# Local heads loaded as fp32 by the hardware queues, crossbar transposes from batch 3, P v with [v|1], and MoE tiles of 256 tokens

## The chip, the cores and the metric

The kernel runs on one core of one Trainium2 chip. The metric is the device time of one execution, in microseconds (us); lower is better. Two runs of the kernel before took 360.77 and 363.22 us, median 362.0 us. "Slow" means over 1.5% above the fastest run of the same kernel in the same series, and only fast runs are compared. TensorE's granted clock is given for each run, 1.0 being full speed.

In the lines of the profile, PE is a matmul on TensorE, PEld a weight load there, DVE is VectorE, ACT ScalarE, POOL GpSimd and SP the Sync engine; L203 is line 203 of the kernel. PSUM, in banks, is the memory that the matmuls write. "The crossbar" is the path by which a DMA transposes on the way (`dma_start_transpose`). "Cold" stands for TensorE at half clock.

The span of a profile (first to last instruction) is about 1.7 us shorter than the time of the same run, so spans are compared with spans and times with times.

## The reference

```python
# q, k, v: (8 batches, 8 heads, 576, 64) fp32
scores = q @ k^T / 8
local   (heads 0..3): 0 <= i - j < 32
strided (heads 4..7): 0 <= i - j and i % 32 == j % 32
attn = softmax(where(mask, scores, -1e9)) @ v
x = attn as (4608 tokens, 512)
h = x @ w_in                       # 512 -> 2048
out = where(h > 0, h, exp(min(h, 0)) - 1) @ w_out   # 2048 -> 512, fp32
```

The matmuls run in bf16. Strided heads are computed residue by residue (8 residues of 72 positions); local heads in blocks of 96 queries against 128 keys.

## The kernel before

All loads go through the GpSimd queue, which casts fp32 to bf16 on the way. Every pair of heads is transposed on TensorE, scored, masked and multiplied by v in "pieces"; one piece is dealt out with each step of the MoE (one tile of the first product, L347, and four matmuls of the second, L382).

```python
def load_qloc(b):                    # cast inside the DMA, GpSimd queue
    t = p_in.tile([RS, 2, NS, 2, D], BF16, tag="ql", name="ql")
    for h in range(HG):
        nc.gpsimd.dma_start(out=t[:, h // 2, :, h % 2, :],
                            in_=q[b, h].rearrange("(p s) d -> p s d", s=NS))
    return t
# ... load_str, load_kloc, load_vloc alike; load_batch calls qs, ks, vs, ql, kl, vl

def piece_T(P):                      # 14 to 16 TensorE transposes, two DVE copies
    for nm, dst in (("q", P.qT[:, 0:S]), ("k", P.kT[:, PRE:PRE + S])):
        ps = p_a.tile([128, S], BF16, tag="a", name="tp")
        # ... nc.tensor.transpose(ps[:, o:o + RS], src..., identity[0:RS, 0:RS])
        nc.vector.tensor_copy(dst, ps)

def piece_S(P, u, split=False):      # scores, exp on ScalarE, mask on DVE
    # ... nc.tensor.matmul(scs[z][...], lhsT=P.kT[...], rhs=P.qT[...])
    nc.scalar.activation(e[0:R], sc[0:R, :, 0:W], ACT.Exp, scale=scale)
    nc.vector.tensor_mul(pm, e, mask)

def piece_O(P, u, pm):               # sums by a matmul with ones, then P v
    nc.tensor.matmul(s_ps[x * D:(x + 1) * D, :], lhsT=ones, rhs=pm[:, x], ...)
    nc.tensor.matmul(o_ps[x * D:(x + 1) * D, i * LQ:(i + 1) * LQ], lhsT=v..., ...)
    # ... rc = exp(-ln(s_ps)) on ScalarE; xT = o_ps * rc on DVE

def l1(nb, m):                       # 128 of d_ff x 512 tokens
    for c in range(KC):
        nc.tensor.matmul(hps, lhsT=w_in_sb[:, cc, m * 128:(m + 1) * 128],
                         rhs=xT[:, cc, nb * CHUNK:(nb + 1) * CHUNK], ...)
    nc.scalar.activation(e, hps, ACT.Exp)
    nc.vector.tensor_scalar(e1, e, scalar1=1.0, scalar2=1.0, op0=ALU.min, op1=ALU.subtract)
    nc.vector.tensor_tensor(g[:, m, :], e1, hps, op=ALU.max)

# order of the start: batch 0's q, k; masks; batch 0's rest; w_in; load_batch(1); w_out;
# batch 0's pieces alone; then, for every MoE step, one piece of the following batches
for nb in range(NCH):
    for m in range(MC):
        if nb > 0: l2(nb - 1, m)
        if done < len(pieces): run_piece(pieces[done], ...); done += 1
        l1(nb, m)
        if loaded < B and done >= (loaded - 1) * PB + 4:
            batch_in[loaded] = load_batch(loaded); loaded += 1
```

The softmax here doesn't subtract the row's maximum and nothing guards it: scores larger than these inputs give would overflow.

## Time and profile before

| | before |
|---|---|
| time, median of 2 | 362.0 us |
| span of the profile | 361.1 us |
| TensorE busy | 329.1 us, 91% |
| first matmul | 6.5 us |
| first MoE tile starts | 36.3 us |
| one batch of attention beside the MoE (12 steps) | 29.85 us |

The page of the kernel before. The second line has the busy time of each engine and its share of the span. In the lower lines each digit is one fortieth of the span (9.0 us), in tenths of busy time; PEclk is the granted clock in tenths, and DMA the mean busy share of the DMA engines.

```profile
span 361.1 us, 6843 instructions
PE 329.1 (91%) x2656; PEld 161.5 (45%) x2656; DVE 243.8 (68%) x501; ACT 194.3 (54%) x377; POOL 92.3 (26%) x120
...
PE   1851986999999999999999999999999999999995
...
PEclk9999999899999999999999999999999999999999
DMA  6999999999959965992960111010111110021122
```

TensorE is at nine tenths from the eighth slice on (63 us): it is the bound, except at the start. The waits of TensorE in the kernel before (engine, line, awaited; then us in total, number of waits, longest):

```profile
PE tp L203 <- DMA qs<-in_q_dram: 18.4, 3, 9.4
PE tp L203 <- DMA ks<-in_k_dram: 3.6, 3, 1.4
```

Nearly all its waiting is for the strided q and k of the first batches. The timeline of TensorE in the steady part (start us, us, engine, line, operation, tiles, count) shows one step, with transposes, and the start of the next:

```profile
101.21 1.04 PE L347 MATMUL hps<-xT,w_in_sb 128*128 128x512 bf16 x4
102.08 1.03 PE L382 MATMUL ops<-w_out_sb,g 128*128 128x512 bf16 x4
103.04 0.31 PE L270 MATMUL s_ps<-pm,ones 72*64 72x288 bf16 x2
103.18 0.30 PE L279 MATMUL o_ps<-pm,vs 72*64 72x72 bf16 x8
103.41 0.43 PE L211 MATMUL tp<-identity,ql 72*128 72x72 bf16 x8
103.85 0.42 PE L211 MATMUL tp<-identity,kl 96*128 96x96 bf16 x6
104.11 1.03 PE L347 MATMUL hps<-xT,w_in_sb 128*128 128x512 bf16 x4
```

The step that starts at 101.21 has four matmuls of the first product, four of the second, two sums, eight P v matmuls, and then 14 transposes before the next step at 104.11. Read durations from start to start, since the ends of pipelined matmuls overlap: four 512-wide matmuls take 0.87 us (101.21 to 102.08). The busy time of the engines in twelve such steps (window, length, then busy time and instructions of PE, PEld, DVE, ACT and POOL, clock, DMA share, GB/s):

```profile
98.83:128.68 29.85, 29.72 (x286) 14.75 (x286) 23.78 (x49) 19.81 (x40) 10.28 (x13) 1.00 0.85 91
```

TensorE works 29.72 of 29.85 us. 96 MoE matmuls of 0.216 us are 20.7 us of it, so that attention costs 9.15 us a batch.

### The profile page before, as it was taken

The numbers are of one execution on the slowest core, as the hardware profiler recorded it, in microseconds if no ns is written. First come the engines' busy times: TensorE is split into PE (matmuls) and PEld (weight loads), VectorE is DVE, ScalarE is ACT, GpSimd is POOL, SyncE is SP. The second block draws the span as 40 slices with busy tenths as digits, with TensorE's granted clock in tenths as the row PEclk, the third lists the DMA queues.
The fourth block names the chain that finished last, engine by engine and source line by source line (L and its number), as shares of the span: only waits on it lengthen the run. The fifth ranks groups of instructions, "written<-read, shape, count | busy, mean of one in ns | idle before, by whom it ended". The sixth has DMA issues, their size and how long they took to land.

```text
span 361.1 us, 6843 instructions
## 1 busy us (share of the span) xinstructions
PE 329.1 (91%) x2656; PEld 161.5 (45%) x2656; DVE 243.8 (68%) x501; ACT 194.3 (54%) x377; POOL 92.3 (26%) x120
## 2 busy tenths in 40 slices
PE   1851986999999999999999999999999999999995
PEld 1630443454544544445454454444444444444442
DVE  2640797787877877777878777776666666666610
ACT  1650575667566666666666666664444433543411
POOL 7952843958507214510620000000000000000000
PEclk9999999899999999999999999999999999999999
DMA  6999999999959965992960111010111110021122
GB/s 91 113 178 178 107 199 158 99 159 152 142 93 102 96 101 72 87 114 63 119 48 29 31 31 31 29 32 29 46 44 30 34 55 29 29 59 31 30 71 76
DMA packets 88321, 29.03 MB, mean 80 GB/s; under 512 B 72672, under 2 KB 83680, under 8 KB 88288
## 3 DMA queue, kind: packets, MB, share of 16 engines
q0 software_dynamic: 82432, 19.14, 61.7%
q1 hardware_dynamic: 5856, 9.44, 9.1%
q8 instruction: 21, 0.34, 0.4%
q14 instruction: 12, 0.10, 0.1%
HBM read 38.21 MB, written 9.44 MB: 132 GB/s over the span
## 4 chain that ended last, share of the span: by engine, by line
PE 73%; DMA 12%; ACT 6%; POOL 4%; issue 2%; DVE 2%; ACTq 0%
PE ops L382 32%; PE hps L347 30%; DMA vs<-in_v_dram 5%; DMA ks<-in_k_dram 5%; PE tp L211 3%; PE tp L203 2%; PE sc L243 2%; ACT e L251 2%; ACT osb L387 2%; DMA vl<-in_v_dram 2%; DVE pm L259 2%; PE s_ps L286 1%; ACT ln L297 1%; PE s_ps L270 1%; POOL kl L85 1%
## 5 line engine op out<-in xcount | busy, mean ns | idle before, releaser
L347 PE MATMUL hps<-xT,w_in_sb 128*128 128x512 bf16 x576 | 151.4, 386 | 0.2
L382 PE MATMUL ops<-w_out_sb,g 128*128 128x512 bf16 x576 | 145.4, 379 | 0.0
L352 ACT ACTIVATE he<-hps 128x512 f32<-128x512 f32 x144 | 85.8, 596 | 103.7 <-PE hps L347 103.0
L382 PEld LDWEIGHTS <-g 128*128 128x128 bf16 x576 | 56.4, 98 | 68.0
L347 PEld LDWEIGHTS <-w_in_sb 128*128 128x128 bf16 x576 | 50.8, 99 | 53.3 <-issue 2.1
L251 ACT ACTIVATE e<-sc 72x576 bf16<-72x576 f32 (+1 forms) x60 | 38.3, 639 | 17.4 <-PE sc L243 17.4
L297 ACT ACTIVATE ln<-s_ps 128x288 f32<-128x288 f32 x64 | 26.3, 411 | 16.9 <-PE s_ps L270 8.7
L387 ACT COPY osb<-ops 128x512 f32<-128x512 f32 x36 | 21.1, 586 | 20.0 <-PE ops L382 20.0
L76 POOL DMA_DIRECT2D ql<-in_q_dram x32 | 27.2, 855 | 18.0 <-PE tp L211 6.6
L299 ACT ACTIVATE rc<-ln 128x288 f32<-128x288 f32 x64 | 28.4, 443 | 2.0
L85 POOL DMA_DIRECT2D kl<-in_k_dram x32 | 23.7, 758 | 19.7 <-DMA ks<-in_k_dram 5.5
L203 PE MATMUL tp<-identity,qs 72*128 72x72 bf16 x128 | 7.9, 213 | 18.4 <-DMA qs<-in_q_dram 18.4
L304 DVE TENSOR_TENSOR xT<-o_ps,rc 128x288 bf16<-128x288 f32 x32 | 14.6, 456 | 8.3 <-ACT rc L299 7.9
L309 DVE TENSOR_TENSOR xT<-o_ps,rc 128x288 bf16<-128x288 f32 x32 | 14.6, 457 | 7.8 <-ACT rc L299 5.0
L253 DVE TENSOR_TENSOR pm<-e,mask_s 72x576 bf16<-72x576 bf16 x32 | 14.5, 452 | 3.8 <-ACT e L251 2.4
L259 DVE TENSOR_TENSOR pm<-e,mask_l 128x576 bf16<-128x576 bf16 x32 | 14.6, 457 | 2.5 <-ACT e L251 0.5
L203 PEld LDWEIGHTS <-qs 72*128 72x128 bf16 x128 | 5.8, 108 | 19.9 <-DMA qs<-in_q_dram 18.7
L67 POOL DMA_DIRECT2D vs<-in_v_dram x8 | 5.7, 710 | 31.9 <-PE sc L243 31.6
L96 POOL DMA_DIRECT2D vl<-in_v_dram x8 | 9.6, 1197 | 11.8 <-PE tp L203 11.4
L286 PE MATMUL s_ps<-pm,ones 128*64 128x288 bf16 x64 | 10.6, 322 | 1.6 <-DVE pm L259 0.9
L203 PE MATMUL tp<-identity,ks 72*128 72x72 bf16 x128 | 7.9, 214 | 3.9 <-DMA ks<-in_k_dram 3.6
L291 PE MATMUL o_ps<-pm,vl 128*64 128x96 bf16 x192 | 10.6, 215 | 0.7 <-DMA vl<-in_v_dram 0.7
(343 smaller groups left out, 338.5 us busy)
## 6 DMA issues: line engine op xcount, KB each, us to landing
out_dram<-osb SPq DMA_DIRECT2D x32, 144.0 KB
qs<-in_q_dram POOLq DMA_DIRECT2D x8, 288.0 KB, 5.9
ks<-in_k_dram POOLq DMA_DIRECT2D x8, 288.0 KB, 7.7
vs<-in_v_dram POOLq DMA_DIRECT2D x8, 288.0 KB, 7.9
ql<-in_q_dram POOLq DMA_DIRECT2D x32, 72.0 KB, 6.3
kl<-in_k_dram POOLq DMA_DIRECT2D x32, 72.0 KB, 4.2
vl<-in_v_dram POOLq DMA_DIRECT2D x8, 288.0 KB, 5.5
w_in_sb<-in_moe_w_in_dram POOLq DMA_DIRECT2D x4, 512.0 KB, 10.9
```

Source lines behind the costliest of these rows:

```text
L76: nc.gpsimd.dma_start(out=t[:, h // 2, :, h % 2, :], in_=q[b, h].rearrange("(p s) d -> p s d", s=NS))
L85: nc.gpsimd.dma_start(out=t[:, h // 2, :, h % 2, :], in_=src[b, h].rearrange("(t p) d -> p t d", p=LQ))
L203: nc.tensor.transpose(ps[:, o:o + RS], src[:, P.g0 + x, 2 * sp * D:2 * (sp + 1) * D], identity[0:RS, 0:RS])
L251: nc.scalar.activation(e[0:R], sc[0:R, :, 0:W], ACT.Exp, scale=scale)
L259: nc.vector.tensor_mul(pm, e, mb.unsqueeze(1).to_broadcast([128, 2, W]))
L297: nc.scalar.activation(ln, s_ps, ACT.Ln)
L299: nc.scalar.activation(rc, ln, ACT.Exp, scale=-1.0)
L304: nc.vector.tensor_mul(dst, o_ps.rearrange(pat, z=2, sp=2), rc.rearrange(pat, z=2, sp=2))
L347: nc.tensor.matmul(hps, lhsT=w_in_sb[:, cc, m * 128:(m + 1) * 128], rhs=xT[:, cc, nb * CHUNK:(nb + 1) * CHUNK], start=(c == 0), stop=(c == ...
L352: nc.scalar.activation(e, hps, ACT.Exp)
L382: nc.tensor.matmul(ops, lhsT=g[:, m, kk * 128:(kk + 1) * 128], rhs=w_out_sb[:, m, :], start=(m == 0), stop=(m == MC - 1))
L387: nc.scalar.copy(o_sb, ops)
```

## The change

The intent was to take work off TensorE: the transposes of batches 3 to 7 go to the DMA crossbar, and the separate matmuls for the row sums go away by multiplying with [v|1] in the array's free columns. Local heads come as fp32 over the Sync and ScalarE queues in one load each and are cast on GpSimd. MoE tiles of 256 tokens (two 128-wide slices of d_ff in one PSUM bank) let the MoE begin when batch 0 alone is finished; 16 of these tiles run before batch 1's attention. The core of the diff:

```diff
-CHUNK = 512
+SUB = 256
+RP = 80
...
-    def load_qloc(b):
-        t = p_in.tile([RS, 2, NS, 2, D], BF16, tag="ql", name="ql")
-        for h in range(HG):
-            nc.gpsimd.dma_start(...)
+    def load_ql(b, eng):
+        eng.dma_start(out=ql32..., in_=q[b, 0:HG].rearrange("h (t p) d -> p (h t) d", p=LQ))
...
+    def dma_T(b, which):            # qs, ks, ql, kl -> qsT, ksT, qlT, klT
+        nc.sync.dma_start_transpose(out=out_.rearrange("p (c n) -> p c n", n=n), in_=in_)
...
+    def piece_O(b, hp, u, pm):      # two banks: [o|sum] and [sum|o]
+        o = [p_a.tile([128, W], F32, tag="a", name=f"o{x}") for x in range(2)]
+        for x, c, vt, mv in pv_terms(b, hp, u, pm):
+            nc.tensor.matmul(o[x][:, c], lhsT=vt[:, x * D:(x + 2) * D], rhs=mv, ...)
+        nc.scalar.activation(ln[lo], o[0][hi], ACT.Ln)
+        nc.scalar.activation(ln[hi], o[1][lo], ACT.Ln)
+        nc.scalar.activation(rc, ln, ACT.Exp, scale=-1.0)
+        x_out(b, hp, u, lo, o[0], rc)          # DVE multiply, 64 partitions
+        x_out(b, hp, u, hi, o[1], rc)
+    def piece_O2(b, hp, u, pm):     # sums apart, as before; batches 0 and 1
...
+    def l1(j, t, mode="A", spare=False):
+        for mm in range(2):
+            for c in range(KC):
+                nc.tensor.matmul(hps[:, mm], lhsT=w_in_sb[... stride 4 ...],
+                                 rhs=xT[:, c, r0:r0 + SUB], ...)
+        nc.scalar.activation(e, hps, ACT.Exp)
+        if mode == "B":
+            nc.scalar.activation(e1, hps, ACT.Relu)
+            nc.vector.scalar_tensor_tensor(gt, e, 1.0, e1, op0=ALU.subtract, op1=ALU.min)
+        else:
+            eng = nc.gpsimd if mode == "P" else nc.vector
+            eng.tensor_scalar(e1, e, scalar1=1.0, scalar2=1.0, op0=ALU.min, op1=ALU.subtract)
+            nc.vector.tensor_tensor(gt, e1, hps, op=ALU.max)
...
+    # start: batch 0's loads, casts, v casts on GpSimd, then w_in; batch 0's attention;
+    load_str(1, qs, q); load_str(1, ks, k); load_str(1, vs, v)
+    load_kl(1, nc.scalar); load_ql(1, nc.scalar); load_vl(1, nc.scalar)
+    # ... batch 1's casts on GpSimd; w_out
+    for n, (j, t) in enumerate(first):         # 16 tiles of batch 0
+        l1(j, t, mode="BP"[n % 2], spare=n % 3 == 2)
+    for it in att_T(1, "O2"):
+        do(it)
+    # ... then 128 steps "n": one tile of l1 and four matmuls of l2 each, with the attention
+    # of batches 2 to 7 dealt among them; START = {3: 22, 4: 34, 5: 50, 6: 67, 7: 84}
```

## The prediction

> **What bounds it now.** The page gives TensorE 91% busy, its 40 slices over 90% from about 62 to 356 us: TensorE-bound except at the ends. In the timeline after 242 us (MoE only) a 128x512 matmul starts every 0.216 us; 1152 make 248.5 us. In steady state (chain of waits, 98.83 to 128.68 us) twelve steps, one batch of attention, take 29.85 us; 96 MoE matmuls are 20.7, so attention costs TensorE 9.15 us a batch, 73 in all. Sum 322 of 361 us. The other 39: 6.5 before the first matmul, 4 after the last, the rest before 62 us, where the waits view names DMA (18.4 us for q, 3.6 for k, strided heads, behind the weights in the GpSimd queue) and matmuls run cold (four 512-wide ones 1.9 us, not 0.86).
>
> **TensorE.**
> - Transposes leave it for batches 3 to 7. A step without them takes 2.44 us, 1.73 of it MoE: score plus P v cost 0.71, eight 5.7 a batch, four transposes the other 3.45. 5 x 3.45 = 17 us saved.
> - P v with [v|1]: separate sum matmuls (0.12 to 0.15 us) go in 48 pieces of batches 2 to 7. The o_ps matmuls already take their serial time (six of 96 columns in 0.24 us), so full width adds nothing. About 5 us saved (0.10 each).
> - 256-token tiles: same columns, 576 more matmuls. The Trainium skill, "TensorE: Matmul & The Clock Gate", section "Wait — 56ns, not 53.3ns?", gives N / 2.4 GHz + about 2.5 ns; 0.216 us for 512 agrees. Estimate from it: +1.4 us. Weight loads now stride by four elements; transposes here reload 128-column weights every 0.03 us, so I expect them hidden under 0.109 us.
>
> Net -21 us, all on the critical path in steady state.
>
> **Other engines.** A batch, DVE loses 8 copies (0.45 us) and gains 8 output multiplies (0.457): even; ACT gains 8 Ln (0.41). Estimate per steady batch of 18 steps (about 35 us): DVE 31 us, ACT 29; DVE has 12% slack. GpSimd casts (eight a batch, about 1.2 us each, from 1.03 for 128x576) share its SBUF port with DVE (Trainium skill, "SBUF — State Buffer": an exclusive lock for the whole instruction; before's one 1.10 us DVE minimum among 0.42 us ones may be that). I allow 4 us of bubbles: DVE, PSUM banks (P v takes two of three), late transposes.
>
> **Startup.** Batch 0 starts later (first matmul near 11 us, after local q, k land as 256-byte pieces and are cast), then 16 MoE tiles of batch 0 need only w_in, then batch 1's attention runs with no MoE beside it (about 14 us for 9 of work). About 32 us of TensorE work done at 62 us, against 29 before: 3 gained. Larger runs for w_out and three queues may give 5 more. Tail unchanged.
>
> **Predicted time.** 362 - 21 - 3 - 5 + 4, rounded down: 334 us, range 318 to 352. Faster by over 2%: 0.86; within: 0.10; slower: 0.04.
>
> **What would show each step.** Transposes only of batches 0 to 2 in the groups; 18 steady steps near 35 us. 256-wide matmuls starting every 0.109 us when nothing waits; 0.12 or more means exposed strided weight loads. No s_ps after batch 1. TensorE continuously busy from about 60 us. No scores waiting for DMA transposes.
>
> **What would make it wrong.** Exposed strided weight loads (+10% is 12 us); crossbar transposes so slow that scores wait at each batch's start; stores stuck behind them in the Sync queue; DVE or ACT becoming the bound through strided output multiplies or GpSimd's lock; a startup slower than before because 256-byte fp32 loads come first.

## The result, and the profile after

The changed kernel took 387.56 us (386.77 and 388.35) against 362.0 us in the same series: the ratio is 1.070, 95% interval 1.060 to 1.080. A ratio is always the mean time of one kernel's fast runs over that of the other's of the same rounds, so it is not quite the ratio of the medians quoted. A faster kernel, 334 us, had been predicted; it is 7% slower than before.

The page of the changed kernel (one slice is 9.7 us):

```profile
span 386.6 us, 7373 instructions
PE 318.0 (82%) x2783; PEld 225.5 (58%) x2824; DVE 264.9 (69%) x488; ACT 221.7 (57%) x433; POOL 98.8 (26%) x108
...
PE   0575117676997779997999999999999999999995
...
PEclk9999658855899999999999999999999999999999
DMA  9789999005010996998919988995946111101111
```

TensorE did less (318.0 us busy, although much of the start ran at half clock; some matmul records are missing in this trace), and it stays under nine tenths in the first ten slices (97 us), where in before it is there from the eighth slice on (63 us). PEclk falls to five and six tenths in four of them. TensorE's waits in the changed kernel:

```profile
PE hps L316 <- DVE g L332: 15.4, 12, 9.5
PE tp L199 <- DVE qlb L116: 12.7, 1, 12.7
PE hps L316 <- ACT he L327: 7.2, 1, 7.2
```

The first wait is mainly one of 9.5 us for the activation of an early MoE tile; the second is the load and cast of batch 0 before the first matmul at 12.73 us; the third is one wait for ScalarE. The windows view of the changed kernel by stage (columns as in before): the start up to the main loop's step 0, steps 0 to 12, 12 to 18, 18 to 108, and the tail:

```profile
0.00:94.24 94.24, 46.02 (x496) 35.84 (x496) 45.52 (x79) 38.62 (x76) 49.49 (x52) 0.79 0.80 136
94.24:118.40 24.16, 22.97 (x172) 16.49 (x172) 15.53 (x31) 9.73 (x17) 1.31 (x2) 0.90 0.08 22
118.40:149.80 31.40, 25.66 (x245) 15.79 (x245) 19.31 (x40) 19.76 (x41) 9.18 (x11) 1.00 0.75 126
149.80:339.60 189.80, 181.59 (x1612) 128.97 (x1640) 161.17 (x300) 136.96 (x272) 38.84 (x44) 1.00 0.71 124
339.60:386.60 47.00, 41.74 (x268) 28.37 (x271) 23.39 (x42) 16.63 (x28) 0.00 (x0) 0.99 0.16 46
```

The granted clock in the start is 0.79 by this view, which overstates it: the trace has no clock record before 37.8 us, and the view takes that as full clock, but six transposes of 96 columns took 0.46 us there (12.73 to 13.19) against 0.26 in the steady part of before. The record itself has half clock from 41.2 to 61.7 us and from 75.4 to 99.2. (The start of before was cold as well, up to about 41 us: four 512-wide matmuls took 1.8 us at 36.32.) The main loop begins at 94.24 us. The work done by then (attention of batches 0 and 1 at 9.15 us each and 16 tiles at 0.87) is 32.2 us of TensorE at full clock. The kernel before has 28.7 us of it done when its 13th tile starts, at 62.27 us, and the other 3.5 would bring it to about 66 us. So the start costs 28 us more than in before, and the remaining 292.4 us are only some 3 us fewer than before's remaining 295. The difference of the spans, 25.5 us, is the sum of the two. There are two misses to explain, then: a start that grew, and a steady part that hardly shrank.

What ScalarE did when TensorE first waited for it, in the changed kernel's timeline (ACTq rows are DMA issues on ScalarE's queue; the bracket is the idle time before and what ended it):

```profile
30.25 6.98 ACTq L96 DMA_DIRECT2D ql<-in_q_dram  x1
37.32 3.92 ACTq L106 DMA_DIRECT2D vl<-in_v_dram  x1
41.28 2.99 ACTq L107 DMA_DIRECT2D vl<-in_v_dram  x1
44.32 0.60 ACT L324 ACTIVATE he<-hps 128x512 f32<-128x512 f32 x1 [14.00 <-issue]
```

The last attention activation ended near 30.3 us. The next, the exponential of the first MoE tile, ran at 44.32, after 14.00 us in which ScalarE's queue did nothing but issue the rest of batch 1's local loads. GpSimd in the same stretch (POOL rows):

```profile
41.86 0.82 POOL L116 CAST klb<-kl 96x768 bf16<-96x768 f32 x1 [12.04 <-DMA kl<-in_k_dram]
...
52.01 2.05 POOL L126 COPY vsx<-vs 72x1024 bf16<-72x1024 bf16 x2
54.01 3.87 POOL L331 TENSOR_SCALAR he<-he 128x512 bf16<-128x512 f32 x2
```

It waits for those loads until 41.86 us, casts and copies until 54.0, and only then runs the min/subtract of the first MoE tiles given to it, 1.94 us each, where VectorE takes 0.456. TensorE, whose PSUM banks wait to be emptied, stands still until 56.77 us.

The steady part of the changed kernel, in an undisturbed stretch (to be read against the timeline of before):

```profile
245.27 0.30 PE L220 MATMUL sc<-qsT,ksT 64*128 64x72 bf16 x8
245.50 1.07 PE L316 MATMUL hps<-xT,w_in_sb 128*128 128x256 bf16 x8
246.40 1.03 PE L356 MATMUL ops<-w_out_sb,g 128*128 128x512 bf16 x4
247.27 0.42 PE L266 MATMUL o<-pm,vsx 72*128 72x72 bf16 x8
247.53 1.04 PE L316 MATMUL hps<-xT,w_in_sb 128*128 128x256 bf16 x8
```

Eight 256-wide matmuls take 0.90 us (245.50 to 246.40), P v with [v|1] 0.26 (247.27 to 247.53), scores 0.23, and there are no transposes. That is as expected, and a step averages 2.04 us in such stretches; but steps 18 to 108 took 189.80 us, 2.109 each. At the starts of batches TensorE waits for chains of score, exponential, mask and P v.

### The profile page after: what moved, and what is told of

It is laid out like the page before. It is cut to its first block, busy times and chain, and to the rows that moved or that the text cites. A ratio compares the mean times of both kernels' runs of the same rounds, so it can differ in the third digit from the quotient of the medians.

```text
span 386.6 us, 7373 instructions
## 1 busy us (share of the span) xinstructions
PE 318.0 (82%) x2783; PEld 225.5 (58%) x2824; DVE 264.9 (69%) x488; ACT 221.7 (57%) x433; POOL 98.8 (26%) x108
## 4 chain that ended last, share of the span: by engine, by line
PE 56%; DVE 14%; ACT 9%; issue 5%; DMA 5%; POOL 4%; SPq 3%; ACTq 3%; DVEq 0%; POOLq 0%
PE hps L316 25%; PE ops L356 24%; DVE xT L244 3%; DMA vl<-in_v_dram 3%; PE sc L220 3%; DVE g L332 3%; POOL he L331 2%; ACT e L223 2%; DVE he L331 2%; ACT osb L361 2%; ACTq L96 2%; SPq L96 2%; PE o L266 1%; PE tp L199 1%; DMA qlT<-qlb 1%
## 5 line engine op out<-in xcount | busy, mean ns | idle before, releaser
L316 PE MATMUL hps<-xT,w_in_sb 128*128 128x256 bf16 x1152 | 156.1, 282 | 26.2 <-DVE g L332 15.4
L316 PEld LDWEIGHTS <-w_in_sb 128*128 128x128 bf16 x1152 | 124.0, 116 | 45.6 <-issue 24.3
L332 DVE TENSOR_TENSOR g<-he,hps 128x512 bf16<-128x512 bf16 x136 | 93.5, 687 | 31.4 <-POOL he L331 18.0
L331 DVE TENSOR_SCALAR he<-he 128x512 bf16<-128x512 f32 x128 | 58.3, 456 | 34.0 <-ACT he L324 32.7
L223 ACT ACTIVATE e<-sc 128x576 bf16<-128x576 f32 (+1 forms) x64 | 41.3, 646 | 19.7 <-PE sc L220 18.0
L244 DVE TENSOR_TENSOR xT<-o,rc 64x288 bf16<-64x288 f32 x48 | 32.2, 670 | 7.8 <-ACT rc L272 7.0
L116 POOL CAST klb<-kl 96x768 bf16<-96x768 f32 x14 | 11.9, 849 | 84.5 <-DMA kl<-in_k_dram 84.5
L269 ACT ACTIVATE ln<-o 64x288 f32<-64x288 f32 x48 | 19.6, 408 | 13.8 <-PE o L266 13.4
L240 DVE TENSOR_TENSOR xT<-o,rc 64x288 bf16<-64x288 f32 x48 | 21.8, 454 | 5.1 <-ACT rc L272 4.0
L270 ACT ACTIVATE ln<-o 64x288 f32<-64x288 f32 x48 | 19.4, 404 | 2.3 <-PE o L266 1.2
L126 POOL COPY vsx<-vs 72x1024 bf16<-72x1024 bf16 x16 | 17.6, 1129 | 1.6 <-DMA vs<-in_v_dram 1.6
L120 POOL CAST vlx<-vl 128x768 bf16<-128x768 f32 x16 | 14.1, 908 | 13.9 <-DMA vl<-in_v_dram 13.3
L331 POOL TENSOR_SCALAR he<-he 128x512 bf16<-128x512 f32 x8 | 15.8, 1994 | 5.9 <-ACT he L324 5.9
```

The costliest lines, as they stand in the source:

```text
L240: nc.vector.tensor_mul(xs[:, u * W:(u + 1) * W], o[pr], rc[pr])
L244: nc.vector.tensor_mul(dst, o[pr].rearrange(pat, b=3, s=NS), rc[pr].rearrange(pat, b=3, s=NS))
L269: nc.scalar.activation(ln[lo], o[0][hi], ACT.Ln)
L316: nc.tensor.matmul(hps[:, mm], lhsT=w_in_sb[:, c, (m // 4) * 512:(m // 4 + 1) * 512].rearrange("c (p mm) -> c mm p", mm=4)[:, m % 4], rhs= ...
L331: eng.tensor_scalar(e1, e, scalar1=1.0, scalar2=1.0, op0=ALU.min, op1=ALU.subtract)
L332: nc.vector.tensor_tensor(gt, e1, hps, op=ALU.max)
```

## The experiments

Eighteen kernels ran. All computed the right result but one, which is told. The medians and ranges quoted are of all runs of a kernel, the ratios of its fast runs alone; e10, e12, e13 and e14 have one slow run each, and e6, e7, e16 and e18 are told below. "Before" was run beside each; it took 361.2 to 362.7 us (medians) throughout. The "main loop's start" below is the time of the first tile of step 0 in the profile, 94.24 us in the changed kernel.

### The start: who issues, who computes

**e1_sp_loads**: batch 1's local loads are issued on the Sync queue.

```diff
-    load_kl(1, nc.scalar); load_ql(1, nc.scalar); load_vl(1, nc.scalar)
+    load_kl(1, nc.sync); load_ql(1, nc.sync); load_vl(1, nc.sync)
```

> Edit: only batch 1's three local fp32 loads are issued by the Sync engine instead of ScalarE. Theory A (two gates in a row: ScalarE held 14 us by issuing the loads, then the MoE tiles that go through GpSimd held until its casts end at 54 us): ScalarE is free at 30 us, but the second tile still waits for GpSimd, so the time stays within 5 us of 387.6 (383 to 388). Rival B (the 14 us on ScalarE is the whole loss of the startup): about 373. Rival C (startup is bound by the arrival of bytes): no change, 387.

Measured: 382.25 us (380.19 to 384.32), ratio 1.057 [1.051, 1.063], just below the range of theory A; the main loop starts at 87.7 us. The wait for ScalarE (7.2 us) is gone; in its place the first tiles wait 8.2 us for w_in, which now shares the DMA engines with the earlier loads, and 5.6 us at the next tiles for the activation that GpSimd does.

**e2_no_pool**: the first tiles do not use GpSimd for the activation.

```diff
-        l1(j, t, mode="BP"[n % 2], spare=n % 3 == 2)
+        l1(j, t, mode="BA"[n % 2], spare=n % 3 == 2)
```

> Edit: only the eight of the first sixteen MoE tiles that put their min/subtract on GpSimd put it on VectorE. Theory A: TensorE restarts for good when ScalarE comes free at 44 us, no 9.5 us wait and no pace of 1.94 us a GpSimd tile, so the first sixteen tiles end near 60 us instead of 72 and batch 1's attention starts some 12 to 16 us earlier: about 373. Rival B (ScalarE's block is the whole loss): within 3 us of 387. Rival C (arrival of bytes): within 3 us of 387, since batch 1's attention would wait for its data instead.

Measured: 375.58 us (374.97 to 380.07), ratio 1.041 [1.034, 1.048]; the main loop starts at 80.95 us. The wait for ScalarE stays at 7.3 us, while the one for the activation falls from 15.4 to 7.3 in all (longest 1.5). GpSimd's place in the chain was worth 12 us.

**e3_both**: both edits.

> Edit: both of the above. Theory A: tiles run as soon as w_in is there (33 us), end near 50 us, batch 1's attention then waits a little for its casts (47 to 54 us now), so batch 1 ends some 20 to 26 us earlier than 94 us: 361 to 368. Rival B: 373, as with the loads alone. Rival C (arrival of bytes): at most 5 us gained over the better of the two single edits, and DMA named in the waits before 70 us.

Measured: 370.63 us (367.55 to 372.68), ratio 1.022 [1.015, 1.029]; main loop at 77.4 us. The gains nearly add: 5.3 and 12.0 apart, 16.9 together. The time is above the 361 to 368 us of theory A, and what rival C expected of this run is there too: 5.0 us gained over the better single edit, and DMA named, in a wait of 7.5 us for w_in. So with the two gates gone, the arrival of data counts as well. What is left beside it is batch 1's attention, which runs alone from 58 to 77 us.

**e5_interleave**: on top of e3, batch 1's 24 attention items are dealt three to a tile among the last eight of the first 16 tiles.

```diff
+    seq1 = att_T(1, "O2")
     for n, (j, t) in enumerate(first):
-        l1(j, t, mode="BA"[n % 2], spare=n % 3 == 2)
-    for it in att_T(1, "O2"):
-        do(it)
+        l1(j, t, mode="BA"[n % 2], spare=n < 8 and n % 3 == 2)
+        if n >= 8:
+            for it in seq1[3 * (n - 8):3 * (n - 7)]:
+                do(it)
```

> Edit: on top of both startup edits (370.6), batch 1's 24 attention pieces are dealt out among the second eight of the first sixteen MoE tiles, three a tile, instead of following them alone. If TensorE in that stretch (58 to 77 us) waits on the chain score, exp, mask, P v and runs cold, as the timeline suggests, MoE work hides it: 6 to 10 us faster (361 to 365). If the stretch waits for batch 1's data instead (rival C), within 2 us of 370.6.

Measured: 364.51 us (361.71 to 367.1), ratio 1.007 [0.999, 1.015]; main loop at 70.4 us. Attention with MoE work beside it costs 6 us less than attention alone; for this stretch rival C is out.

**e6_early_w_in**: on top of e5, w_in is issued ahead of the casts of batch 0's v.

```diff
-    for a in range(2):
-        cast_v(nc.gpsimd, 0, a)
     for i in range(2):
         nc.gpsimd.dma_start(out=w_in_sb[:, :, i * 1024:(i + 1) * 1024], ...)
+    for a in range(2):
+        cast_v(nc.gpsimd, 0, a)
```

> Edit: on top of the interleaving, w_in is issued from the GpSimd queue before the two casts of v, which wait for v until 17.7 us; now it is issued at 19.5 us. If the first MoE tiles wait for w_in because it is issued late, they start near 30 us instead of 37.6 and the kernel is 3 to 7 us faster than the interleaved one. If the startup is bound by bytes, batch 0's v arrives later by as much and the gain is under 2 us.

Measured: 356.69, 358.25, 367.15 and 368.54 us; the last two count as slow. In the profile, that of the fastest run (span 354.9), the main loop starts at 62.7 us. The two groups of times do not differ by clock (0.983 to 1.0 in all), so something in the start, probably how batch 0's v and w_in share the DMA engines, decides each time. That is argued, not shown.

The five runs settle the first miss: the loop's start moved from 94.24 to 87.7, 80.95, 77.4, 70.4 and, in e6's fast runs, 62.7 us, and the time by nearly the same amounts.

### TensorE's terms

**e7_pe_transposes**: in the changed kernel, batches 3 to 7 are transposed on TensorE, two transposed tiles in each of four steps.

```diff
-        at(st - 3, lambda b=b: Ts(b))
+        Tb = [("T", b, p, w, None) for p in range(4) for w in "qk"]
+        for i in range(4):
+            at(st - 2 + i, lambda i=i, Tb=Tb: [do(it) for it in Tb[2 * i:2 * i + 2]])
```

> Edit: on the changed kernel, batches 3 to 7 are transposed by TensorE (two transposes a step, as batch 2 is) instead of the crossbar; nothing else. My prediction: 3.45 us of TensorE a batch, 17 in all: about 404. Theory E (stalls at batch starts come with the crossbar's queue: scores or mask waits there): the gain of the crossbar is partly lost already, so undoing it costs less, 5 to 12 us (393 to 400). If the crossbar were the cause of the slowdown: faster than 387.

Measured: fast runs 411.07, 416.16 and 416.7 us, ratio 1.146 [1.135, 1.156]; the profiled run took 516.44 us at a clock of 0.667, so its profile is not used. Undoing the crossbar costs 24 to 29 us, more than the expectation on either side. So it is not TensorE's time alone. The copies out of PSUM come back to VectorE too; that they make the difference is not shown, for want of a fast profile.

**e4_all_o2**: the sums are computed apart in all batches, as in before.

```diff
-                pend.append(("O", b, p, u))
+                pend.append(("O2", b, p, u))
```

> Edit: batches 2 to 7 use the old P v (separate sums by 64-column matmuls, one Ln, one output multiply) instead of [v|1] at full width. My prediction: full width saves about 0.10 us a piece, 5 us in 48, so undoing it makes the kernel about 5 us slower (392). Theory D (full width takes two PSUM banks and two output multiplies a piece, and the bubbles this makes eat its gain): 3 to 8 us faster (380 to 384), with VectorE busy about 15 us less and fewer waits of P v on VectorE.

Measured: 384.99 us (384.83 to 385.21), ratio 1.064 [1.060, 1.069], 2.6 us faster than the changed kernel. In undisturbed stretches a step takes 2.16 us against 2.04 on average, and one with a P v piece 2.23 against 2.02, so the full width saves TensorE about 0.21 us a piece, twice what was predicted. But steps 12 to 18, into which batch 2 is packed, took 27.8 us instead of 31.4, which is more than the whole difference, and steps 18 to 108 took 190.7 us instead of 189.8: of the 8.4 us that 0.21 makes in 40 pieces only 0.9 was kept. The waits of TensorE in steps 18 to 108, all of e4's and the two longest of the changed kernel's, which sum to 6.4 us:

```profile
PE sc L220 <- ACT e L223: 0.7, 1, 0.7
```

```profile
PE hps L316 <- DVE g L332: 3.3, 9, 0.7
PE o L266 <- DVE pm L225: 1.6, 1, 1.6
```

So nearly all waiting in the steady part comes with the full-width form, as theory D had it; VectorE's busy time fell by 22.1 us over the whole run (264.9 to 242.8). Whether the extra multiplies and Ln make the waits, or TensorE's shorter work no longer covers chains that were there before, is not separated.

### VectorE, casts and the shared port

**e9_casts_twice**: the casts and copies on GpSimd are done twice for batches 3 to 7.

```diff
-        at(st - 5, lambda b=b: casts(b))
+        at(st - 5, lambda b=b: (casts(b), casts(b)))
```

> Edit: on the changed kernel, GpSimd does all its casts and spreads of batches 3 to 7 twice (about 8 us more of GpSimd a batch, 42 in all; result the same). If GpSimd's lock on the shared SBUF port is what makes the steady bubbles (single mask multiplies of 1 to 4 us instead of 0.45 while casts run): those long VectorE instructions double, and it is 4 to 10 us slower. If it is only lateness of the transposes: slower too, but with scores waiting for crossbar transposes and no more long VectorE instructions. If neither: within 2 us of 387.

Measured: 413.39 us (410.78 to 415.31), ratio 1.140 [1.132, 1.147]. The group of VectorE's min/subtract in this run (busy us, mean ns of one, then idle time before):

```profile
L331 DVE TENSOR_SCALAR he<-he 128x512 bf16<-128x512 f32 x128 | 76.0, 594 | 36.4 <-ACT he L324 35.2
```

It was 456 ns on average in the changed kernel, and 594 here, with single ones longer by 3.7 to 5.0 us. This fits the Trainium skill, "SBUF — State Buffer", section "SBUF: two separate sides": VectorE (in a two-port mode, or with two SBUF inputs against a GpSimd instruction that reads SBUF) and GpSimd share a port pair by an exclusive lock held for the whole instruction. The changed kernel shows one case directly, in VectorE's timeline and then in GpSimd's:

```profile
87.47 3.79 DVE L225 TENSOR_TENSOR pm<-e,mask_s 72x576 bf16<-72x576 bf16 x1 [0.30 <-ACT e L223]
```

```profile
87.04 0.84 POOL L116 CAST klb<-kl 96x768 bf16<-96x768 f32 x1
87.81 0.83 POOL L116 CAST qlb<-ql 96x768 bf16<-96x768 f32 x1
...
90.12 1.82 POOL L120 CAST vlx<-vl 128x768 bf16<-128x768 f32 x2
```

A mask multiply (two SBUF inputs) that takes 0.45 us elsewhere lasted 3.79, from 87.47 to 91.26, while GpSimd ran casts from 87.04 to 91.94. The 26 us are more than the 4 to 10 expected; TensorE waited for no transposes in this run, so their lateness is out.

**e11_cast_in_dma**: batches 3 to 7 are loaded and cast by the GpSimd queue straight into the final tiles; the casts are gone.

```diff
-        at(st - 7 if b == 3 else st - 9, lambda b=b: loads(b))
-        at(st - 5, lambda b=b: casts(b))
+        at(st - 7 if b == 3 else st - 9, lambda b=b: direct(b))
```

> Edit: on the changed kernel, batches 3 to 7 only: local heads and v are loaded and cast by the GpSimd queue's DMAs straight to their places (as before the change), so GpSimd does no casts or spreads there; crossbar, P v and tiles as changed. If the lock of GpSimd's casts on the shared SBUF port makes the steady bubbles: VectorE's long instructions after 150 us go (excess over the median 10 us in all now, of which 4 at the startup), and 5 to 9 us faster (379 to 383). If smaller DMA pieces make the data late: scores wait for crossbar transposes and it is slower than 387.

Measured: 387.44 us (387.15 to 388.81), ratio 1.070 [1.066, 1.074]: no change. The time by which VectorE's instructions after 150 us exceeded their medians fell from about 5 to about 2 us, and the waits did not shrink with it. So the lock is real but, at one set of casts a batch, it is not what holds the steady part. That twice as many no longer fit into VectorE's slack is the likely reading of e9, and is not shown. The expectation of a gain was wrong.

**e8_query_order**: local queries are taken in the order of residues by a stride of eight in the scores' moving operand, so that the output multiply reads PSUM contiguously.

```diff
-                    lhsT, rhs = klT[i_][pr, o:o + 128], qlT[i_][pr, o:o + n]
+                    lhsT = klT[i_][pr, o:o + 128]
+                    rhs = qlT[i_][pr, o:o + n].rearrange("c (p s) -> c s p", s=NS)
...
-            pat = "c (b p s) -> c b s p"
+            pat = "c (b s p) -> c b s p"
```

> Edit: on the changed kernel, local scores take the queries in residue order (the moving operand then steps by eight elements), so the output multiply reads PSUM and the reciprocals in runs, as before the change. The multiply's 0.67 us should fall to about 0.46, VectorE's busy time by about 10 us. If VectorE's load is what makes the steady bubbles (8 us of TensorE idle between 150 and 340 us): 3 to 6 us faster (382 to 385). If strided moving reads slow TensorE, the local scores get longer than 0.24 us a piece and it is no faster.

Measured: 391.73 us (391.0 to 393.46), ratio 1.083 [1.077, 1.089], 4 us slower, though the multiply fell from 0.670 to 0.455 us and VectorE's busy time by 12 us in all. The edit brought a cost of its own on TensorE, in its timeline:

```profile
188.43 0.68 PE L221 MATMUL sc<-qlT,klT 64*128 64x96 bf16 x6
189.05 1.07 PE L317 MATMUL hps<-xT,w_in_sb 128*128 128x256 bf16 x8
```

Six score matmuls now take 0.62 us (188.43 to 189.05), where they took 0.23 to 0.24. Twenty local pieces in steps 18 to 108 make that 7.6 us, and those steps grew by 4.3, so by this sum some 3 us of waiting went away. The experiment does not separate the two cleanly, and the question of VectorE's load stays half open.

### The crossbar alone, on the kernel before

**e10_before_crossbar**: the kernel before with crossbar transposes from batch 3 on, the two extra row groups padded by GpSimd at each load.

```diff
+RP = 80
+XB = 3
-        t = p_in.tile([RS, HG, NS * D], BF16, tag=name, name=name)
+        t = p_in.tile([RP, HG, NS * D], BF16, tag=name, name=name)
+        nc.gpsimd.memset(t[64:RP], 0.0)
...
+            nc.sync.dma_start_transpose(out=dst.rearrange("p (c n) -> p c n", n=n), in_=s)
...
-            pieces.append(("T", pairs[i + 1], 0))
+            pieces.append(("T" if P.b < XB else "-", pairs[i + 1], 0))
```

> Edit: the kernel before, with only the crossbar transposes from batch 3 (inputs still cast by the GpSimd queue's DMAs, strided and local q padded to 80 rows, old P v, old 512-token tiles, old startup). My prediction's term for the crossbar alone: 3.45 us a batch, 17 in all: 344 to 348. If data is not there in time, scores wait at batch starts for transposes, and it stays above 350. If crossbar transposes slow the weights' and inputs' DMAs: 358 or more.

Measured: 371.97 us (370.0 to 375.7), ratio 1.024 [1.015, 1.034]. The first activation of the MoE came 7.3 us later than in before (45.5 against 38.3 us), behind the padding writes on GpSimd of 1.80 us each, and the scores waited 7.4 us for the transposed keys.

**e12_before_crossbar2**: padding once, on VectorE, and loads eight pieces earlier. The result was wrong (relative error 0.465): batch 4 was loaded over tiles of batch 2 that the program still had to read. 

```diff
-            if loaded < B and done >= (loaded - 1) * PB + 4:
+            if loaded < B and done >= (loaded - 1) * PB - 4:
```

> Edit: the kernel before with only the crossbar, mended: the padding rows are zeroed once by VectorE instead of each batch by GpSimd, q and k are loaded some eight steps earlier, transposes are issued three to four steps earlier. The first try lost 8.5 us at the start to padding and 7.4 us to scores waiting for transposes. If those were what hid the gain: 344 to 350. If it is still over 356, the crossbar's gain on this kernel is not the 17 us that I predicted.

Measured: 424.35 us; nothing follows from it.

**e14_before_crossbar3**: the same, mended: early loads only for q and k and only where both batches use the crossbar; v later.

```diff
+            if loaded < B and done >= (loaded - 1) * PB + (4 if loaded < XB + 2 else -4):
+                load_batch(loaded, "qkv" if loaded < XB + 2 else "qk")
```

> Edit: the kernel before with only the crossbar, with the mistake of the second try mended (it loaded batch 4 over batch 2's tiles while TensorE still had to transpose them). Padding rows zeroed once; loads of q and k from batch 5 on eight steps earlier. Crossbar term as predicted (17 us): 344 to 350. If half of it is lost to waits for late data: 350 to 356. If the crossbar gives nothing on the kernel before: 358 or more.

Measured: 358.28 us (356.15 to 364.68), ratio 0.986 [0.982, 0.989]. The first MoE tile came at 39.9 us instead of 36.3, behind the padding, and the scores of batch 3 waited 4.7 us for their keys. Later batches took 26.97 us for twelve steps, against 29.84 in before (counted by the starts of the MoE exponentials).

**e16_before_crossbar4**: crossbar from batch 4; the padding is written by VectorE just ahead of the loads of batches 4 and 5, nothing at the start.

```diff
-XB = 3
+XB = 4
-    for n, i in pads[:3]:
-        pad(n, i)
+        if b in (XB, XB + 1):
+            for n in ("qs", "ks", "ql"):
+                pad(n, b % 2)
```

> The kernel before with the crossbar transposes alone, from batch 4 on, and nothing added at the start: the zero padding of the transposed tiles is written by VectorE just ahead of the loads of batches 4 and 5. Theory (the crossbar itself is worth 2.6 to 2.9 us of TensorE for each batch, and the earlier attempts lost it again at the start and in one wait at batch 3): four batches give 10.4 to 11.6 us, so 350 to 352 us, with the first MoE tile where it is in before (about 36.3 us) and no wait of the scores for the transposed keys over 1 us. Rival (the crossbar's DMA crowds the other loads or VectorE's long padding writes hold up a tile, so part is given back whenever it is used): 355 to 360 us.

Measured: 369.77 us (362.83 to 373.69); two of six runs are fast (362.83 and 367.49), their ratio 1.007 [1.001, 1.014], and the profiled run is a slow one. Its record of waits and of GpSimd's loads:

```profile
PE sc L290 <- DMA xks<-ks: 13.0, 2, 10.6
```

```profile
134.90 0.75 POOL L80 DMA_DIRECT2D qs<-in_q_dram  x1 [22.68 <-PE sc L290]
```

Batch 5's first load went out only at 134.90 us, no earlier than in before and behind the padding on VectorE (133.38 to 134.29). The transpose of its keys followed at 146.18 and landed at 164.5, 10.6 us after the scores needed it. This run missed the 351 us expected by 19. The one wait of 10.6 us is the largest part; a second for keys (2.4 us) and waits of the sums for VectorE's masks (5.4 us), of which 4.8 fall at the two paddings, make up most of the rest, so the rival held in part. All this is seen in a slow run only. Batches 6 and 7 took 26.97 and 26.62 us in the same run. So the lead time and the padding were the suspects, and the next kernel takes both away.

**e17_before_crossbar5**: the padding is copied once by six small transfers on the idle Sync queue after batch 0's attention, and q and k of all four crossbar batches are loaded early.

```diff
     def pad(n, i):
-        nc.vector.memset(IN[n][i][64:RP], 0.0)
+        p = "p h c -> p (h c)" if n[1] == "s" else "p a t h d -> p (a t h d)"
+        nc.sync.dma_start(out=IN[n][i][RS:RP].rearrange(p), in_=z8)
...
-            if loaded < B and done >= (loaded - 1) * PB + (4 if loaded < XB + 2 else -4):
+            if loaded < B and done >= (loaded - 1) * PB + (4 if loaded < XB else -3):
```

> The crossbar on the kernel before from batch 4 on, once more, with the two things mended that the previous run showed: the padding is copied once, by six small transfers on the idle Sync queue just after batch 0's attention, instead of by VectorE ahead of batches 4 and 5; and those batches' queries and keys are loaded early like the later ones, so that the transposes have the same lead for all four. Theory (27.0 and 26.6 us for a steady batch, as batches 6 and 7 had in the previous run, against 29.85 in before, and nothing lost elsewhere): four batches times 2.8 to 3.2 us give 349 to 352 us, and the wait of the scores for the transposed keys is under 1 us in all. Rival (the crossbar's transfers crowd the loads, so that one wait or the other comes back wherever it starts): 355 us or more.

Measured: 350.82 us (348.96 to 351.84, six fast runs), ratio 0.968 [0.964, 0.971]: faster by over 2% than before, and within the expected range. The page of this run:

```profile
span 348.8 us, 6327 instructions
PE 313.2 (90%) x2375; PEld 151.6 (43%) x2416; DVE 232.9 (67%) x468; ACT 193.8 (56%) x377; POOL 92.2 (26%) x120
...
PE   1850877999999999999999999999999999999995
...
PEclk9999999899999999999999999999999999999999
```

Twelve steps of a crossbar batch (to be read against the 29.85 us of before, columns as there):

```profile
148.31:175.28 26.97, 26.29 (x221) 12.33 (x224) 20.99 (x41) 19.72 (x39) 10.03 (x13) 1.00 1.30 147
```

The first three crossbar batches gain 2.88 us each and the last 2.54 (26.62 against 29.16), 11.2 in all; the spans differ by 12.3. No wait for transposed keys is left in the list of TensorE's waits. This is the fastest kernel.

**e18_crossbar_from2**: the same with the crossbar from batch 2.

```diff
-XB = 4
+XB = 2
```

> The previous kernel with the crossbar from batch 2 on instead of batch 4: six batches in place of four, nothing else changed. Theory (a crossbar batch is about 2.9 us cheaper than one with TensorE transposes, as 362.4 minus 350.8 us over four batches says, and the loads are on time): 350.8 minus 5.8 gives 345 us. Rival (batch 2's early loads and the crossbar's transfers fall among the loads of the MoE weights and batch 1, and the startup pays for it as in the changed kernel): 350 us or more, with the scores waiting for batch 2's transposed keys or the first MoE tiles for weights.

Measured: 364.31 us (355.33 to 367.74). Five of six runs are slow. The waits in the profiled (slow) run:

```profile
PE sc L290 <- DMA xks<-ks: 12.5, 2, 11.9
PE sc L290 <- DMA xkl<-kl: 5.7, 2, 4.2
```

In this run it is the rival's picture: batch 2's strided k was issued at 43.99 us behind w_out and landed at 60.5, its transposes followed, and the scores waited 11.9 us. Even the one fast run is 4.5 us above e17's median, and there is no profile of it. As built, the gain did not go on to batches whose loads fall among the loads of the start; for a fast run the cause is not shown.

### The changed kernel, mended

**e13_mended**: e6 with the casts of batches 2 to 7 in the DMA, as in e11.

```diff
-    at(1, lambda: loads(2))
-    at(7, lambda: casts(2))
+    at(1, lambda: direct(2))
...
-        at(st - 5, lambda b=b: casts(b))
```

> Edit: the changed kernel with all that helped: loads off ScalarE, first tiles off GpSimd, batch 1 interleaved, w_in issued early, and batches 2 to 7 cast by the DMA. From the sum of the single effects: 357 minus 5 to 9, so 346 to 352, faster than both kernels. If the casts' lock is not the steady loss: 355 to 360.

Measured: 362.31 us (357.99 to 365.41), ratio 0.993 [0.985, 1.001]. Batch 0's v landed at 24.5 us, beside w_in, and P v waited 5.5 us for its cast; the main loop began at 70 us. In e6's fast profile v landed at 19.0. Both expectations, 346 to 352 and 355 to 360, were missed.

**e15_mended2**: in e13, half of w_in is issued after the casts of v.

```diff
+    nc.gpsimd.dma_start(out=w_in_sb[:, :, 0:1024], in_=w_in_v[:, :, 0:1024])
     for a in range(2):
         cast_v(nc.gpsimd, 0, a)
+    nc.gpsimd.dma_start(out=w_in_sb[:, :, 1024:2048], in_=w_in_v[:, :, 1024:2048])
```

> Edit: the mended changed kernel, with only the first half of w_in issued before the casts of v, the second half after. In the mended kernel batch 0's v landed at 24.5 us, in the best profile of the early-w_in kernel at 19.0, and P v waited 5.5 us; if w_in crowding v on the DMA engines makes that difference, v lands near 19 to 20 us always, and the time is 354 to 359 with a smaller spread. If not: 358 to 365 as before.

Measured: 360.23 us (359.23 to 364.45), ratio 0.996 [0.992, 1.000]: v landed near 22.6 us and the wait fell from 5.5 to 3.5, but the medians differ by 2 us only, less than either kernel scatters; w_in crowding v is not confirmed. With the start mended as far as I got, the changed kernel equals before and stays 9 us behind e17.

## Why the prediction was wrong, point by point

**The bound.** Right: TensorE-bound, apart from the start. e17 confirms it: TensorE's saving appeared in full in the time.

**The crossbar, "5 x 3.45 = 17 us saved".** Right in mechanism, too large in size: 2.88 us a batch on the kernel before (e17). The estimate took eight score and P v pieces as 5.7 us a batch; they take 6.3 (26.97 less 20.7), and the timeline before has four groups of transposes at 0.70 us each, 2.8. In the changed kernel the crossbar was worth 24 to 29 us (e7), perhaps because it also spares VectorE's copies there. Its delays were not the loss: the scores of the changed kernel waited for it 0.2 us in all.

**P v with [v|1], "about 5 us saved".** TensorE saves about 0.21 us a piece in undisturbed steps, twice the 0.10 predicted, and yet the sum was wrong: e4 shows 2.6 us lost, because the waits that come with the full width cost more.

**256-token tiles, "+1.4 us", and strided weight loads.** Right: eight matmuls of 256 columns take 0.87 us where nothing waits (0.109 each), as the formula of the Trainium skill's page "TensorE: Matmul & The Clock Gate", section "Wait — 56ns, not 53.3ns?" gives. Loading the stride-four weights took 116 ns on average against 99, and stayed hidden.

**The start: the step that failed.** In the words of the prediction: "About 32 us of TensorE work done at 62 us, against 29 before: 3 gained. Larger runs for w_out and three queues may give 5 more." The 32 us of work were done at 94.24 us, 32 us later, or 37 with the "5 more". The prediction had counted the work and laid it behind the loads. It had not followed who issues the loads, who casts, and who empties PSUM: ScalarE issued loads for 14.0 us with the first MoE activation behind them; GpSimd, whose casts waited for those loads, stood as one of the activation engines of the same tiles; and batch 1's attention then ran alone. e1, e2, e3, e5 and e6 took these away one by one. On top TensorE fell to half clock in the pauses. The Trainium skill, "TensorE: Matmul & The Clock Gate", section "What's actually happening", says that an idle window of about 3.4 us halves the clock until work has been sustained as long again. The first fall here agrees roughly: the clock halved at 41.2 us, 3.0 us into the wait for ScalarE (38.2 to 45.45), and came back at 61.7, 4.9 us after the tiles went on. The second, at 75.4, came 1.9 us into a pause of 3.4 that followed only 1.2 us of work.

**"I allow 4 us of bubbles".** Mis-sized. From the prediction's own sum the part after the loop's start should take 322 - 21 - 32 of work, 4 after the last matmul and 4 of bubbles: 277 us. It took 292.4, so the bubbles were about 19 us. Set against the TensorE work in each stage at full pace (estimates from the contents of the steps: about 20.7, 24.0 and 181.4 us, the last being 90 steps of 1.74 and 40 pieces of 0.62), steps 0 to 12 lost about 3.5 us, of which 2.5 are the half clock up to 99.2 us, steps 12 to 18, with batch 2's pieces packed into six steps, 7.4, and steps 18 to 108 lost 8.4. The cause that the prediction named, GpSimd's lock on VectorE, is not it (e11). Neither is late crossbar data. The full-width P v is most of it: with the old form TensorE waits 0.7 us instead of 6.4 in steps 18 to 108, and steps 12 to 18 take 3.6 us less although TensorE has more to do (e4). The prediction had asked of the wider matmul only whether it costs TensorE time. That the waits lie where attention is packed at the starts of batches is seen in the steps; which part of the full-width form makes them is open, VectorE's load being at most a part (e8).

**The sum.** 337 us before rounding, 37 for the start and 15 for the bubbles give 389; measured 387.6.

What stays open: why e6, e13, e15 and the kernels with early crossbar loads scatter by 5 to 10 us from run to run, which part of the full-width P v makes TensorE wait, and how much of the stalls at batch starts a different dealing of the pieces would remove. The mended changed kernel with the old P v was not run.

## What to carry to other kernels

Before crediting a startup with "the work is there", write down for each engine the queue of what it issues and computes in that stretch: one load issued on a computing engine's queue, or one helper engine that must first finish something else, holds the whole chain. Change one term at a time: here the crossbar, one of four changes, is the only one for which a gain in time was shown (the fp32 loads and the 256-token tiles were not tried alone), and by itself, with loads early enough and nothing added to the start, it made the kernel 3.2% faster. A saving on the bounding engine is worth its size only where that engine is kept fed; look at what a wider instruction takes from the engines that feed it.

## What the Trainium skill lacked or had wrong

- "DMA: Bandwidth & Descriptors", section "Issuing engines are not separate DMA queues", calls the time to initiate a DMA "usually small relative to the DMA itself". Three local fp32 loads in 256-byte pieces held ScalarE's queue 6.98, 3.92 and 2.99 us here, and its compute 14.0 us in all. The page does not say that an issue can keep the engine's later compute waiting so long; where the skill has the issuing sequencer busy until all descriptors are made, it gives no time near these.
- "GPSIMD Engine Reference", section "4.1 Engine selection", gives about a factor of 2 against VectorE for two-input operations and line rate for one-input ones. The one-input min/subtract of 128x512 fp32 to bf16 took 1.99 us on GpSimd (mean of eight; most 1.92) and 0.456 on VectorE, a factor of 4.4. Waits for the shared port are not excluded.
- "DMA: Bandwidth & Descriptors", section "DMA Transpose (X-bar)", has the constraints but no time. SBUF-to-SBUF transposes held the Sync queue 1.3 to 1.7 us each (96 partitions x 1536 elements) and 1.5 to 2.1 us (80 x 2048) in the changed kernel, and 1.5 to 6.8 us (80 x 2048) in the crowded, slow run e16, where one took 18.3 us from issue to landing.
- "SBUF — State Buffer" names the lock and agrees with 3.79 us for a 0.45 us multiply; that one set of casts a batch cost nothing measurable (e11) while two cost 26 us (e9) is in no page.
- No page gives the size of the cost of a strided moving operand or PSUM read (that leaving a 16-byte line of SBUF, or any non-contiguous PSUM access, costs something is said): six score matmuls of 96 columns took 0.62 us with a stride of eight elements against 0.24 contiguous, and the 64x288 output multiply 0.670 us with strided against 0.454 with contiguous access.
